# Decode attention beside an MLP: V laid out as K is, P's rows picked by 0/1 products and masked, one sum bank per two batches, wo in two tiles behind V

## The chip, the cores and the metric

The kernel runs on one core of one Trainium2 chip. The metric is the device time of one execution in microseconds (us), the median of the runs shown. Beside it stands one execution that the hardware profiler took; its span is what the profile's pages count from.

## The reference

One decode step (one new token for each of 4 batches, D = 576) through two branches that are added up. Everything is bf16 at the edges.

```python
xn = layernorm(x)                                   # 4 x 576
out = x + A(xn) + B(xn)
# A: attention over the last W = 2048 rows of a cache of 8192
q = (xn @ wq)                                       # 4 x 32 heads x 128
k, v = k_cache[:, :, Sk-W:], v_cache[:, :, Sk-W:]   # 4 x 16 kv heads x 2048 x 128
p = softmax(q . k / sqrt(128))                      # two q heads share a kv head
A = (p . v).reshape(4, 4096) @ wo                   # wo: 4096 x 576
# B: with S = 1 the shifted parts are zero, so w1 and w2 drop out
B = xn + gelu(layernorm(xn) @ w3) @ w4              # w3: 576 x 4608, w4: 4608 x 576
```

K and V of the window are 33.55 MB each, the weights some 20 MB; all of it is read once.

## The kernel before, in words

**Loads.** Nearly every load is issued from SyncE (SP), in one first-in first-out queue. The order: wq; K in eight tiles with w3 and the first 11 of w4's 36 row blocks between the first ones; V; wo; the rest of w4. A pool `big` of four slots of 32 KB per partition holds, one after the other, wq, the K tiles, w3 and its neighbours, V's tiles and w4's end. A load whose slot is still in use waits in SP, and what stands behind it waits too. `k_load` (line 105) brings a K tile as 128 runs of 32 KB: partition 4m + q holds 128 consecutive rows of one of 32 (batch, head) pairs. `v_load` (line 115) brings a pair of heads in two transfers of 128 runs of 16 KB each: partition 32b + p holds 64 consecutive rows of batch b. wo comes in two transfers in runs of 9,216 B (`load_wo`, line 404), the first between V's pairs 1 and 2, the second behind V.

**Scores.** For each K tile VectorE transposes blocks of 32x32 (line 296, four instructions), and TensorE (PE) multiplies (line 303), 32 columns of the array at a time, four such strips side by side. The scores of all 128 rows (32 heads x 4 batches) build up in four PSUM banks S0 to S3, 512 columns each. Beside that stage PE does w3 (line 486) and the first part of w4 (line 394).

**Softmax** (line 308). The maximum of each bank (line 315), their maximum as a bias `nb` (317), exponentials on ScalarE into f32 (320) with row sums, reciprocals (325). P is then scaled by the reciprocals times a 0/1 mask of the batch (lines 339 and 341), transposed on PE (345), and copied into `PZ` (350, 353), where a head's weights lie as 32 columns.

**V.** `v_compute` (line 374) multiplies each head's 64 chunks with PZ: 16 matmuls of 512 columns, in four strips of 32 columns that run side by side, into a bank of its own (383). `head_out` (418) takes the four diagonal blocks out of that bank on VectorE (423, 425); a product with `sel` transposes and sums them (435), and for each four heads products with `pick` (446) and VectorE (454, 455) bring the rows into the order that wo's tile has. wo's products run between the heads (`project`, 459). PE's order in this stage is written out by hand (line 552); the other engines are scheduled by the framework.

**The end.** `merge_sums` (468) folds the partial sums into four accumulators, one for each quarter of the 576 columns; `quads` (413) issues four narrow matmuls for a row block. w4's end arrives last, in ever smaller pieces (570, 502, 577); four copies (594) and two output transfers (596) follow.

Of the kernel before, what the change touches and what calls it, by code (L numbers as in the profile page):

```python
# [20 lines left out]
def kernel(  # L21
# [19 lines left out]
    nc = tc.nc  # L41
# [10 lines left out]
    NCH = W // G  # L52
    NG = P // G
    GK = G // B
    NY = 4
    CP = 16
    NP = NCH // CP
    assert NCH * GK == 512
# [12 lines left out]
    v_win = A_v_cache[:, :, Sk - W:Sk, :]  # L71
# [41 lines left out]
    V_tiles = {}  # L113

    def v_load(pair):
        t = big.tile([P, 2, NCH, Dh], BF16, tag="big", name=f"v{pair}")
        for i in range(2):
            h = 2 * pair + i
            nc.sync.dma_start(out=t[:, i, :, :].rearrange("p c d -> p (c d)"),
                              in_=v_win[:, h].rearrange("b (p c) d -> p b (c d)", p=G))  # L120
            V_tiles[h] = t[:, i, :, :]
# [7 lines left out]
    XR = 8  # L129
    wo_src = A_wo.rearrange("(g p x) n -> p g (x n)", p=P, x=XR)  # L130

# [17 lines left out]
    K_order = [(bp, kq) for bp in range(2) for kq in range(4)]  # L149
    K_tiles = {0: k_load(*K_order[0])}  # L150
# [47 lines left out]
    NH = Hkv * rep  # L198
    qz = pzp.tile([P, 2, NM, NY, G], BF16, tag="pz", name="qz")

    mask = const.tile([P, B], F32)
    nc.vector.tensor_reduce(out=mask[:], in_=ident[:].rearrange("p (h b r) -> p b h r", b=B, r=rep), op=ALU.add, axis=AX.XY)
# [12 lines left out]
    ACCS = [ACC]  # L215
# [66 lines left out]
    S = []  # L282

    def k_scores(n):
# [8 lines left out]
        for i in range(4):  # L293
            e, a = divmod(i, 2)
            c0 = a * C2 // 2
            nc.vector.transpose(out=ap32(kt[e], c0 * 2 * G, [[2 * G, C2 // 2], [1, 2], [2, G]]),  # L296
                                in_=ap32(kn, c0 * 4 * G + e * G, [[4 * G, C2 // 2], [2 * G, 2], [1, G]]))
        for e in range(2):
            for t in range(2):
                y = 2 * e + t  # L300
                for m in range(NM):
                    c = 32 * (m % 4)
                    nc.tensor.matmul(out=S[kq][c:c + 32, :].rearrange("p (c q l) -> p c q l", q=4, l=2),  # L303
                                     lhsT=qz[:, bp, m, y, :], rhs=kt[e][:, :, 4 * m:4 * m + 4, :, t],
                                     start=(bp == 0 and m < 4 and y == 0), stop=(bp == 1 and m >= 4 and y == NY - 1),
                                     skip_group_check=True)

    def softmax():

        E = ktp.tile([P, NCH, NG, GK], F32, tag="kt", name="E")  # L310
        mx = const.tile([P, NG], F32)
        nb = const.tile([P, 1], F32)
        sm = const.tile([P, 2 * NG], F32)
        for g in range(NG):
            nc.vector.reduce_max(out=mx[:, g:g + 1], in_=S[g][:], axis=AX.X)  # L315
        nc.vector.reduce_max(out=nb[:], in_=mx[:], axis=AX.X)
        nc.vector.tensor_scalar_mul(out=nb[:], in0=nb[:], scalar1=-scale)  # L317
        for g in range(NG):
            for x in range(2):
                nc.scalar.activation(out=E[:, :, g, x:GK:2].rearrange("p (c l) q -> p c q l", l=2),  # L320
                                     in_=S[g][:, 256 * x:256 * (x + 1)].rearrange("p (c q l) -> p c q l", q=4, l=2),
                                     func=ACT.Exp, bias=nb[:], scale=scale, accum_out=sm[:, 2 * g + x:2 * g + x + 1])
        rd = const.tile([P, 1], F32)
        nc.vector.tensor_reduce(out=rd[:], in_=sm[:], op=ALU.add, axis=AX.X)
        nc.vector.reciprocal(out=rd[:], in_=rd[:])
        rdm = const.tile([P, B], F32)
        nc.vector.tensor_scalar_mul(out=rdm[:], in0=mask[:], scalar1=rd[:])  # L327

        PZ = pzp.tile([P, Hkv, NCH, B * rep], BF16, tag="pz", name="PZ")
        HC = CP // 2  # L330
        prs = ktp.tile([P, NP, CP, NG, GK, B], BF16, tag="kt", name="prs")
        for piece in range(NP):
            c0 = piece * CP
            pr = prs[:, piece]
            for b in range(B):
                src = E[:, c0:c0 + CP, :, :].rearrange("p c g k -> p (c g k)")
                dst = pr[:, :, :, :, b].rearrange("p c g k -> p (c g k)")
                if b == 3:
                    nc.scalar.mul(out=dst, in_=src, mul=rdm[:, b:b + 1])  # L339
                else:  # L340
                    nc.vector.tensor_scalar_mul(out=dst, in0=src, scalar1=rdm[:, b:b + 1])  # L341
            for half in range(2):
                tp = ps_s.tile([P, HC, P], BF16, tag="S", name=f"pt{piece}{half}")
                for cc in range(HC):
                    nc.tensor.transpose(out=tp[:, cc, :],  # L345
                                        in_=pr[:, half * HC + cc, :, :, :].rearrange("p g k b -> p (g k b)"),
                                        identity=ident[:])
                c1 = c0 + half * HC
                if half:
                    nc.scalar.copy(out=ap_of(PZ, c1 * B * rep, [[NCH * B * rep, Hkv], [B * rep, HC], [1, B * rep]]),  # L350
                                   in_=ap_of(tp, 0, [[B * rep, Hkv], [P, HC], [1, B * rep]]))
                else:
                    nc.vector.tensor_copy(out=ap32(PZ, c1 * B, [[NCH * B, Hkv], [B, HC], [1, B]]),  # L353
                                          in_=ap32(tp, 0, [[B, Hkv], [NH * B // 2, HC], [1, B]]))
        return PZ


    NI = 4
    NB = B * rep
    sel = const.tile([P, NB], F32)  # L360
    nc.vector.tensor_reduce(out=sel[:], in_=ident[:].rearrange("p (q m) -> p m q", m=NB), op=ALU.add, axis=AX.X)
    diag = const.tile([P, NI], F32)
    nc.vector.tensor_reduce(out=diag[:], in_=ident[:].rearrange("p (j i m) -> p i j m", i=NI, m=NB), op=ALU.add,
                            axis=AX.XY)

    pick = const.tile([P, XR, 2, P // XR], BF16)
    for j in range(2):
        nc.vector.tensor_copy(out=pick[:, :, j, :], in_=ident[:].rearrange("p (m x) -> p x m", x=XR))

    half = const.tile([P, 2], F32)  # L370
    nc.vector.tensor_reduce(out=half[:], in_=ident[:].rearrange("p (q j m) -> p j q m", j=2, m=16), op=ALU.add, axis=AX.XY)
    O_tiles = {}

    def v_compute(h):
        bank = ps_o.tile([P, NI * Dh], F32, tag="O", name=f"O{h}")
        vn = V_tiles.pop(h)
        g0, m = divmod(h, NM)
        hp = 4 * (m % 4) + 2 * (m // 4) + g0
        ns = NCH // (NI * NG)
        for s in range(ns):  # L380
            for j in range(NG):
                c0 = (s * NG + j) * NI
                nc.tensor.matmul(out=bank[G * j:G * j + G, :],  # L383
                                 lhsT=PZ[:, hp, c0:c0 + NI, :].rearrange("p c m -> p (c m)"),
                                 rhs=vn[:, c0:c0 + NI, :].rearrange("p c d -> p (c d)"),
                                 start=(s == 0), stop=(s == ns - 1), skip_group_check=True)
        O_tiles[h] = bank

    def acc_matmuls(lhsT, rhs_cols, half):


        for q in range(2):
            o0 = 64 * half + 32 * q
            nc.tensor.matmul(out=ACCS[half][o0:o0 + B, 0:DH], lhsT=lhsT, rhs=rhs_cols(q * DH, (q + 1) * DH),  # L394
                             start=False, stop=False, skip_group_check=True)

    wo_tiles = {}
    groups = {}
    SUMS = []
    NO = 4  # L400

    wo = wop.tile([P, 2, XR, D], BF16)

    def load_wo(g2, n=1):
        s = g2 % 2
        nc.sync.dma_start(out=wo[:, s:s + n].rearrange("p g x n -> p g (x n)"), in_=wo_src[:, g2:g2 + n, :])
        for i in range(n):
            wo_tiles[g2 + i] = wo[:, s + i]

    selects, projects = [], []  # L410
# [7 lines left out]
    def head_out(h):  # L418


        bank = O_tiles.pop(h)
        osum = ktp.tile([P, Dh], F32, tag="kt", name=f"osum{h}")
        nc.vector.tensor_scalar_mul(out=osum[:], in0=bank[:, 0:Dh], scalar1=diag[:, 0:1])  # L423
        for i in range(1, NI):
            nc.vector.scalar_tensor_tensor(out=osum[:], in0=bank[:, i * Dh:(i + 1) * Dh], scalar=diag[:, i:i + 1],  # L425
                                           in1=osum[:], op0=ALU.mult, op1=ALU.add)

        g4, o = divmod(h, NO)

        def transpose_sum():  # L430
            if o == 0:
                OT = ps_tp.tile([P, NO * NB * (1 + XR)], F32, tag="tp", name=f"OT{g4}")
                groups[g4] = OT, small.tile([P, NO, rep, B], BF16, tag="on", name=f"on{g4}")
            OT, on = groups[g4]
# [5 lines left out]
        def select():  # L440
            if o < NO - 1:
                return
# [184 lines left out]
```

## Time and profile before

| what | value |
|---|---|
| median of 3 runs | 212.45 us (212.43 to 212.53) |
| profiled execution, its own time | 212.51 us |
| its span | 210.7 us |
| PE, busy | 99.7 us (47%), 1099 matmuls |
| VectorE (DVE), busy | 128.0 us (61%) |
| ScalarE (ACT), busy | 18.3 us (9%) |
| read from HBM | 87.17 MB, 414 GB/s over the span |

The profile's page divides the span into 40 slices and gives, for each, the busy share of every engine in tenths, the clock that TensorE was granted and the load of the 16 DMA engines. The chain of waits follows the work that ended last back from its end: each piece is what released the next. The timeline lists instructions in order, merged where they repeat, with start, length and count. A window lists for a stretch the busy time and the count of PE, weight loads, DVE, ACT and POOL, then the granted clock (1.00 is full), the DMA engines' busy share and the bytes per time. PE's lengths overlap, since matmuls are pipelined, so a busy PE is not a full one.

### The profile page before, as it was taken

What the parts mean: (1) busy time and instruction counts of PE and PEld (TensorE: products, weight loads), DVE (VectorE), ACT (ScalarE), POOL (GpSimd) and SP (SyncE); (2) the same over time, 40 slices, a digit from 0 to 9 for tenths busy, and PEclk for the clock granted to TensorE, in tenths of its full rate; (3) what the DMA queues carried; (4) which work ended last, traced back from release to release, by engine and by line L of the source; (5) the groups of instructions that cost most, each with busy time, mean ns of one, the idle gap of its engine ahead of it and who ended that gap; (6) DMA issues with size and microseconds to landing.
All of it is one profiled execution on the core that took longest, in us unless ns stands there. A gap on an engine that the chain in (4) does not pass through costs nothing.

```text
span 210.7 us, 2593 instructions
## 1 busy us (share of the span) xinstructions
PE 99.7 (47%) x1099; PEld 50.6 (24%) x1099; DVE 128.0 (61%) x224; ACT 18.3 (9%) x38; POOL 1.8 (1%) x8
## 2 busy tenths in 40 slices
PE   1433159429803333423333330577489455655564
PEld 0110137408301011101111100553234222221352
DVE  7902692096349898979696960996836552522601
ACT  0003200000000000000000008951000000000011
POOL 2100000000000000000000000000000000000000
PEclk9999999999975555555555555589955785555555
DMA  7999999999999999999999999999999999999991
GB/s 299 398 473 423 397 462 395 422 435 470 417 411 473 407 417 467 411 423 460 411 407 426 432 420 414 432 442 423 426 429 426 425 432 417 429 432 411 422 402 60
DMA packets 6002, 87.32 MB, mean 414 GB/s; under 512 B 604, under 2 KB 1128, under 8 KB 1896
## 3 DMA queue, kind: packets, MB, share of 16 engines
q1 hardware_dynamic: 5976, 87.17, 97.3%
q8 instruction: 8, 0.13, 0.2%
q14 instruction: 2, 0.02, 0.0%
q10 hardware_dynamic: 16, 0.01, 0.0%
HBM read 87.17 MB, written 0.00 MB: 414 GB/s over the span
## 4 chain that ended last, share of the span: by engine, by line
DMA 60%; DVE 25%; PE 6%; issue 3%; ACT 3%; SPq 1%; DVEq 0%; ACTq 0%
DMA k<-in_A_k_cache_dram 32%; DVE kt L296 19%; DMA w_end<-in_B_w_dram 16%; DMA v<-in_A_v_cache_dram 12%; PE S L303 4%; DVE prs L341 4%; ACT E L320 2%; PE O L383 1%; DVE PZ L353 1%; PE pt L345 1%; SPq L136 1%; ACT PZ L350 0%; DVE osum L425 0%; SPq L140 0%; PE SUM L415 0%
## 5 line engine op out<-in xcount | busy, mean ns | idle before, releaser
L296 DVE STREAM_TRANSPOSE kt<-k 128x2048 int32<-128x2048 int32 x32 | 71.1, 2281 | 16.2 <-DMA k<-in_A_k_cache_dram 16.1
L303 PE MATMUL S<-kt,qz 128*32 128x512 bf16 x256 | 30.4, 622 | 58.7 <-DVE kt L296 58.7
L383 PE MATMUL O<-v,PZ 128*32 128x512 bf16 x256 | 26.0, 531 | 12.2 <-DMA v<-in_A_v_cache_dram 11.5
L303 PEld LDWEIGHTS <-qz 128*32 128x32 bf16 x256 | 9.4, 126 | 75.6 <-issue 69.2
L423 DVE TENSOR_SCALAR osum<-O,diag 128x128 f32<-128x128 f32 x16 | 5.6, 349 | 23.3 <-PE O L383 23.3
L425 DVE SCALAR_TENSOR_TENSOR osum<-O,diag,osum 128x128 f32<-128x128 f32 x48 | 16.4, 345 | 0.8
L383 PEld LDWEIGHTS <-PZ 128*32 128x32 bf16 x256 | 7.2, 118 | 20.9 <-DMA v<-in_A_v_cache_dram 9.5
L320 ACT ACTIVATE E<-S,nb 128x256 f32<-128x256 f32 x8 | 4.5, 703 | 72.2 <-DVE nb L317 72.2
L345 PE MATMUL pt<-ident,prs 128*128 128x128 bf16 x64 | 6.0, 273 | 9.3 <-DVE prs L341 9.3
L435 PEld LDWEIGHTS OT<-sel,osum 128*128 128x128 f32 x32 | 6.7, 261 | 13.8 <-DVE osum L425 7.9
L435 PE MATMUL OT<-sel,osum 128*128 128x8 f32 x32 | 8.2, 329 | 3.3 <-DVE osum L425 3.3
L345 PEld LDWEIGHTS <-prs 128*128 128x128 bf16 x64 | 5.4, 126 | 10.8 <-ACT prs L339 9.4
L341 DVE TENSOR_SCALAR prs<-E,rdm 128x512 bf16<-128x512 f32 x12 | 7.9, 801 | 0.0
L315 DVE TENSOR_REDUCE mx<-S 128x1 f32<-128x512 f32 x4 | 2.8, 691 | 8.0 <-PE S L303 8.0
L486 PEld LDWEIGHTS <-w3a 128*128 128x128 bf16 x108 | 6.9, 164 | 1.7 <-issue 1.7
L486 PE MATMUL ACC<-ln2T,w3a 128*128 128x4 bf16 x108 | 7.0, 202 | 0.0
L251 DVE CAST q_rows<-qp 128x256 bf16<-128x256 f32 x4 | 1.5, 420 | 8.8 <-PE qp L236 6.7
L394 PE MATMUL ACC<-wo,onx 128*4 128x288 bf16 x48 | 3.4, 434 | 5.6 <-DVE onx L455 5.0
L236 PE MATMUL qp<-wq,xnT 128*8 128x512 bf16 x32 | 3.6, 626 | 3.9 <-DMA wq<-in_A_wq_dram 3.9
L470 ACT COPY sums<-ACC 64x288 f32<-64x288 f32 x1 | 0.4, 392 | 57.0 <-PE ACC L394 57.0
L594 DVE CAST fin<-ACC 4x144 bf16<-4x144 f32 x1 | 0.3, 299 | 7.7 <-PE ACC L415 7.7
L339 ACT ACTIVATE prs<-E,rdm 128x512 bf16<-128x512 f32 x4 | 4.9, 1408 | 0.8 <-DVE rdm L327 0.8
(93 smaller groups left out, 79.0 us busy)
## 6 DMA issues: line engine op xcount, KB each, us to landing
k<-in_A_k_cache_dram SPq DMA_DIRECT2D x8, 4096.0 KB, 29.6
v<-in_A_v_cache_dram SPq DMA_DIRECT2D x16, 2048.0 KB, 25.0
wo<-in_A_wo_dram SPq DMA_DIRECT2D x2, 2304.0 KB, 32.5
wq<-in_A_wq_dram SPq DMA_DIRECT2D x1, 4096.0 KB, 12.7
w3a<-in_B_w_dram SPq DMA_DIRECT2D x1, 2304.0 KB, 26.9
w3b<-in_B_w_dram SPq DMA_DIRECT2D x1, 2304.0 KB
w_end<-in_B_w_dram SPq DMA_DIRECT2D x1, 2016.0 KB, 34.3
w3b<-in_B_w_dram SPq DMA_DIRECT2D x1, 1584.0 KB
```

Source lines behind the costliest of these rows:

```text
L236: nc.tensor.matmul(out=qp[32 * i:32 * i + 2 * B, :], lhsT=x[:, B - B * k:3 * B - B * k], rhs=rhs, start=False, stop=False, skip_group_chec ...
L296: nc.vector.transpose(out=ap32(kt[e], c0 * 2 * G, [[2 * G, C2 // 2], [1, 2], [2, G]]), in_=ap32(kn, c0 * 4 * G + e * G, [[4 * G, C2 // 2], ...
L303: nc.tensor.matmul(out=S[kq][c:c + 32, :].rearrange("p (c q l) -> p c q l", q=4, l=2), lhsT=qz[:, bp, m, y, :], rhs=kt[e][:, :, 4 * m:4 * ...
L320: nc.scalar.activation(out=E[:, :, g, x:GK:2].rearrange("p (c l) q -> p c q l", l=2), in_=S[g][:, 256 * x:256 * (x + 1)].rearrange("p (c q ...
L339: nc.scalar.mul(out=dst, in_=src, mul=rdm[:, b:b + 1])
L341: nc.vector.tensor_scalar_mul(out=dst, in0=src, scalar1=rdm[:, b:b + 1])
L345: nc.tensor.transpose(out=tp[:, cc, :], in_=pr[:, half * HC + cc, :, :, :].rearrange("p g k b -> p (g k b)"), identity=ident[:])
L383: nc.tensor.matmul(out=bank[G * j:G * j + G, :], lhsT=PZ[:, hp, c0:c0 + NI, :].rearrange("p c m -> p (c m)"), rhs=vn[:, c0:c0 + NI, :].rea ...
L423: nc.vector.tensor_scalar_mul(out=osum[:], in0=bank[:, 0:Dh], scalar1=diag[:, 0:1])
L425: nc.vector.scalar_tensor_tensor(out=osum[:], in0=bank[:, i * Dh:(i + 1) * Dh], scalar=diag[:, i:i + 1], in1=osum[:], op0=ALU.mult, op1=AL ...
L435: nc.tensor.matmul(out=OT[:, NB * o:NB * o + NB], lhsT=osum[:], rhs=sel[:], start=True, stop=True, skip_group_check=True)
L486: nc.tensor.matmul(out=gp[:, fc, :], lhsT=lhsT, rhs=rhs, start=False, stop=False, skip_group_check=True)
```

## The change

V is loaded as K is: partition 4m + q holds 128 consecutive rows of a (batch, head) pair, in 32 KB runs, eight tiles of 32 pairs and a quarter of the window each. A chunk c of a V tile thus has 32 pairs on its partitions, and P's weights for it are 64 columns (two heads per pair), zero where row and column belong to different pairs.

- The exponentials go to bf16, unscaled, one instruction per bank (512 columns). 0/1 products with `pick` bring the rows of two batches onto the partitions that V's pairs have (`pick_rows`), ScalarE copies them (`keep_rows`), and VectorE spreads each value over 32 columns and keeps it in its own one by an AND with a mask of all ones or zeros (`spread_rows`). The scaling by batch, the 64 transposes and PZ are gone.
- `v_compute` takes two chunks at a time: 128 weight columns, 256 moving ones, all into one bank per two batches; of the result the two diagonal blocks are used. The last half of the last tile takes single chunks, 64 columns wide, two side by side.
- The scaling by the reciprocals happens once per two batches (`heads_out`), with the reciprocals brought into row order by a product (`reciprocal_rows`); f32 products and a mask bring the rows into wo's order (`heads_rows`, `heads_pick`).
- wo comes in two tiles, in runs of 18,432 B, both behind V and behind the middle of w4. All of wo's products run near the end, with `quads`.
- The bank maxima stand in the source between K's transposes. The hand-written order now covers PE, ScalarE and VectorE.
- The second accumulator of wo and w4 (ACC2) is gone.

The core of the diff:

```diff
-    def v_load(pair):
-        t = big.tile([P, 2, NCH, Dh], BF16, tag="big", name=f"v{pair}")
-        for i in range(2):
-            h = 2 * pair + i
-            nc.sync.dma_start(out=t[:, i, :, :].rearrange("p c d -> p (c d)"),
-                              in_=v_win[:, h].rearrange("b (p c) d -> p b (c d)", p=G))
+    v_rows = A_v_cache.rearrange("b h s d -> (b h) s d")
+    def v_load(n):
+        bp, kq = V_order[n]
+        t = big.tile([P, CK, Dh], BF16, tag="big", name=f"v{n}")
+        lo = Sk - W + kq * 4 * CK
+        src = v_rows[MT * bp:MT * bp + MT, lo:lo + 4 * CK, :].rearrange("m (q c) d -> m q (c d)", q=4)
+        nc.sync.dma_start(out=t[:].rearrange("p c d -> p (c d)"), in_=src)
...
-    XR = 8
-    wo_src = A_wo.rearrange("(g p x) n -> p g (x n)", p=P, x=XR)
+    XR = 16
+    wo_src = A_wo.rearrange("(t p x) n -> p t (x n)", p=P, x=XR)
...
             nc.vector.transpose(out=ap32(kt[e], ...), in_=ap32(kn, ...))
+            if n > 4 and i == 1:
+                bank_max(n - 5)
...
+    def pick_rows(bp, g0, g1):
+        for r in range(rep):
+            ...
+            for q in range(4):
+                nc.tensor.matmul(out=CPS[bp, r][:, g0 * CK:g1 * CK], lhsT=pick[:, bp, r, 3 - q:3 - q + P],
+                                 rhs=EP[:, g0:g1, q, :], start=(q == 0), stop=(q == 3), skip_group_check=True)
+    def keep_rows(bp, g0, g1):
+        for r in range(rep):
+            nc.scalar.copy(out=CB[:, bp, g0:g1, :, r],
+                           in_=CPS[bp, r][:, g0 * CK:g1 * CK].rearrange("p (g c) -> p g c", c=CK))
+    def spread_rows(n):
+        bp, g = V_order[n]
+        X = ktp.tile([P, CK, PB], BF16, tag="kt", name=f"X{n}")
+        src = CB[:, bp, g].rearrange("p c r -> p (c r)").bitcast(I32)
+        for a in range(NX):
+            s32 = src[:, a * CX:(a + 1) * CX]
+            nc.vector.tensor_tensor(out=ap32(X, a * CX * MT, [[MT, CX], [1, MT]]),
+                                    in0=bass.AP(s32.tensor, s32.offset, [list(s32.ap[0]), [1, CX], [0, MT]]),
+                                    in1=ap_of(own, 0, [[0, CX], [1, MT]]), op=ALU.bitwise_and)
+    def v_compute(n, parts=range(NX), narrow=NX):
+        ...
+        for c in range(parts[0] * CX, (parts[-1] + 1) * CX, 2):
+            if c >= narrow * CX:
+                for j in range(2):
+                    nc.tensor.matmul(out=o[PB * j:PB * j + PB, Dh * j:Dh * j + Dh], lhsT=X[:, c + j, :],
+                                     rhs=vn[:, c + j, :], start=False, stop=False, skip_group_check=True)
+            else:
+                nc.tensor.matmul(out=o[:], lhsT=X[:, c:c + 2, :].rearrange("p c n -> p (c n)"),
+                                 rhs=vn[:, c:c + 2, :].rearrange("p c d -> p (c d)"),
+                                 start=(g == 0 and c == 0), stop=False, skip_group_check=True)
...
+        for n in range(1, NV):
+            v_compute(n, narrow=NX // 2 if n == NV - 1 else NX)
+            if n == 1:
+                pick_rows(1, 0, NG)
+                keep_rows(1, 0, NG)
+                reciprocal_rows()
+            if n == 2:
+                merge_sums()
+            if n == 3:
+                heads_out(0)
+            if n + 1 < NV:
+                spread_rows(n + 1)
+            if n == 4:
+                heads_pick(0, heads_rows(0))
+            if n - 1 + NV0 < NV:
+                V_tiles[n - 1 + NV0] = v_load(n - 1 + NV0)
+            if n == NV - NV0 + 1:
+                ...
+                wo.append(load_wo(0, wop, "wo"))
+                wo.append(load_wo(1, big, "big"))
+        heads_out(1)
+        for part in end[:2]:
+            quad_out(*part)
+        heads_pick(1, heads_rows(1))
+        for t in range(NT):
+            for x in range(XR):
+                quads(onx[:, t, x, :], wo[t][:, x, :])
+        for part in end[2:]:
+            quad_out(*part)
```

`heads_rows` is four f32 matmuls of 128 columns, `heads_pick` three VectorE instructions (a product with a 0/1 mask over 512 columns, a reduction, a copy into bf16).

## The prediction

> **What bounds the kernel now.** I read the page's slices first, then the windows by stage, the chain that ended last and the timeline of PE.
>
> ```profile
> span 210.7 us, 2593 instructions
> ...
> PEclk9999999999975555555555555589955785555555
> DMA  7999999999999999999999999999999999999991
> ...
> q1 hardware_dynamic: 5976, 87.17, 97.3%
> ```
>
> The DMA row is full in every slice but the first and the last, and the queue's packets fill 97.3% of the 16 engines' span. So the end is set by 87.17 MB through engines that never rest; a saving on any other engine is worth nothing unless that engine is late at the very end. The chain agrees: its last long pieces are transfers.
>
> ```profile
> 114.67 8.89 DVE kt L296 x4
> ...
> 126.47 0.16 DVE nb L317
> ...
> 126.70 4.56 ACT E L320 x16
> ...
> 148.68 25.04 DMA v<-in_A_v_cache_dram
> 173.72 0.02 issue
> 173.74 33.22 DMA w_end<-in_B_w_dram
> 206.95 0.04 issue
> 207.00 0.28 PE SUM L415
> ```
>
> Columns are start, length, what. The last piece of w4 lands at 206.95, PE ends 1.3 us later, and the span ends 2.5 us after PE, with copies and the output. Two windows compare a stretch of nothing but K with one of nothing but V; two more show what the granted clock does.
>
> ```profile
> 62.00:108.00 46.00, 15.44 (x132) 5.01 (x135) 40.26 (x21) 0.00 (x0) 0.00 (x0) 0.50 1.00 431
> 136.00:192.00 56.00, 36.62 (x372) 17.73 (x369) 32.18 (x109) 4.70 (x5) 0.00 (x0) 0.68 1.01 426
> ...
> 149.10:152.50 3.40, 1.71 (x27) 0.96 (x26) 2.87 (x13) 0.00 (x0) 0.00 (x0) 0.99 1.02 434
> 154.50:161.60 7.10, 7.10 (x62) 2.90 (x58) 3.30 (x11) 0.00 (x0) 0.00 (x0) 0.50 1.02 432
> ```
>
> The last three columns are clock, DMA share and GB/s. With the engines full in both, K (32 KB per partition and transfer) moves at 431 GB/s, V (16 KB) at 426.
>
> **The change, part by part.**
>
> *V's runs.* 16 transfers of 16 KB runs become 8 of 32 KB runs, the shape of K's, in the same slots. 33.55 MB at 426 GB/s are 78.8 us, at 431 GB/s 77.9: **-0.9 us**. The trace's record of single packets says nearly the same: 2048 packets of 16 KB with a median of 613 ns against 1024 of 32 KB with K's 1214 ns, over 16 engines, are 78.5 and 77.7 us (-0.8); by means (617 and 1219 ns) -1.0.
>
> The Trainium skill ("DMA: Bandwidth & Descriptors", Specifications) puts line rate at transfers of 512 B and more; by it both run lengths are at full rate and this part is worth 0. The two windows, 426 and 431 GB/s, disagree with it by 1.2%.
>
> *wo's runs.* 512 packets of 9,216 B (median 352 ns) become 256 of 18,432 B. w3 has packets of that length now: 686 ns. 512 x 352 / 16 = 11.26 us against 10.98: **-0.25 us**, by means -0.2. Both wo tiles move behind V, to where the queue is as full.
>
> *The queue's order.* SP waits for V4's slot (V0 through PE), V5's, and so on. K4 lands at 80.1 by the chain, so K7 lands at 80.1 + 3 x 9.73 (4.19 MB at 431) = 109.3, and V tile n at 119.0 + 9.73 n. wo no longer stands between V1 and V2, so the four tiles that are issued early are used up at 148.2 and V4 must be issued by about 146. V7 lands at 187.1, then w4's middle, wo, w4's end.
>
> *Softmax and P.* Gone: 16 scalings with 0/1 masks, 64 transposes, 8 copies into PZ. The bank maxima stand in the source between K's transposes, but in the built program's order VectorE still has each ahead of the next tile's transposes, as before; so nb is still done at 126.6, and nothing is gained there. New: the first exponential (512 wide; the row for 256 wide is 0.70 us, spaced 0.54; I take 0.8), 4 products of 128 columns per bank, their copies (0.35 each, by 0.375 for 128x256), and the AND, 1024 int32 wide. No row shows an int32 AND. Below, the transposes move 2048 int32 in 2.28 us, 1.1 ns each; above, the product of 144 f32 in 0.31 us is 2.1 ns each with its fixed part. I take 1.2 us, as the fixed part is spread over 1024. A V tile needs four, 4.8 us (at most 8.8), under a landing period of 9.73. The first V matmul then starts at about **130.6**.
>
> *PE in the V stage.* This is where the change adds work: per tile 64 matmuls with 128 weight columns and 256 moving ones, one after the other, where 32 of 512 columns ran four side by side. Rows of PE's timeline:
>
> ```profile
> 134.02 3.61 PE L345 MATMUL pt<-ident,prs 128*128 128x128 bf16 x32 [8.52 <-DVE prs L341]
> ...
> 141.04 1.07 PE L345 MATMUL pt<-ident,prs 128*128 128x128 bf16 x16 [0.31 <-DVE prs L341]
> ...
> 145.72 1.05 PE L383 MATMUL O<-v,PZ 128*32 128x512 bf16 x16
> ```
>
> All three change their weights before each matmul. At full clock 16 of 128 columns take 1.07 us, 67 ns each, or 53 when the latency of one (0.27) is taken off; so 107 to 134 ns for 256 columns. The last row is 4 passes of 512 columns in 1.05: 0.22 each without its latency (0.39), 110 for 256. I take **110 ns**. At half clock (first row) it is 226. Does the clock stay full? Those transposes began at 134.0 and the windows give full clock from 139: 4.8 us at half, and then full while PE was dense.
>
> The sum from 130.6: 480 wide matmuls 52.8; V7's second half as 64 narrow ones, two side by side, 2.6 (40 ns; between the quads' 28 and 57); the picks of P's rows, 8 of 384 and 8 of 512 columns, 3.1; the reciprocals' rows, which PE waits for behind two copies on ScalarE, 1.6 (V2's matmuls are queued behind that wait); the sums' merge 0.5; the f32 products of the first half of the heads 1.5; half of 4.8 us lost to the clock, 2.4. Together 64.5: V7 is done at **195.1**. PE is behind the landings all along, so V4 is asked for at 141 (146 allowed) and no later slot is late.
>
> *The tail.* After V7: 56 quads at 28 ns, 1.6; f32 products 1.5; three steps on VectorE (512 wide, as the 0.69 of L315) 1.75; 128 quads 3.55; 24 quads 0.7. That must end by the landing of w4's last large piece, 206.95 - 1.1 = 205.85; so V7 may be done as late as 205.85 - 9.1 = **196.75**. The slack is 1.65 us, which 508 units of 256 columns use up at 3.3 ns each: the decision point is **113 ns** per matmul, and each ns above it costs 0.5 us. Beyond that the end is as before: the same small w4 pieces, copies and output.
>
> Sum: -0.9 - 0.2 = **-1.1 us**. The profiled execution took 212.51 (span 210.7), 211.4 after; the median shown is 212.45, 0.03% away, so the forecast is 211.4 for both. Cover gone, it is the PE rival's price.
>
> **The rivals.**
>
> *PE sets the end (slower).* The place is V7's end, the price 0.5 us per ns above 113. At the upper end, 134 ns (67 for 128 columns, latency and all), that is +10.5 us, 221.9; I put the likely miss at 120 ns, +3.3: **214.7**. The clock can do it too: every us at half rate loses half a us, so 3.3 us of it use up the slack. For it: the window 149.1 to 152.5 with 1.71 us of work cost the clock, and the next 7 us of gapless work ran at 0.50; if the reciprocals' wait, which leaves some 1.8 us of work in 3.4, did that again for 8 us, PE would lose 4 us, and the end 2.4: 213.8. Against it: the 53 ns that the transposes take without the latency, and 128 full columns in use without a break.
>
> The Trainium skill ("TensorE: Matmul & The Clock Gate", Part 1) has the full clock come back after about 3.4 us of sustained work. By that V0 would lose 1.7 us instead of 2.4; the row of 7.10 us at 0.50 disagrees.
>
> *The rate does not depend on the run's length.* The 5 GB/s would then come from what V's stage does beside the transfers, not from the packets: **212.5**, no change. Against it, the packets' median rates rise with the length across all stages: 9,216 B 26.2 bytes per ns and engine, 16,384 B 26.7, 18,432 B 26.9, 32,768 B 27.0.
>
> *V4 is asked for late.* If the clock stays at half through V0, PE ends it at 130.6 + 64 x 0.226 + 8 x 0.34 = 147.8, 1.8 us after 146: 211.4 + 1.8 = **213.2**, and PE's lateness comes on top.
>
> *The change does not do what it says* in one point, the maxima, counted above. Had they moved, nb would be 4.7 us earlier and PE's slack 6.
>
> **How the numbers follow.** Forecast 0.62 at 211.4 (211.0 to 211.8 by the bounds of the two rates, 210.9 rounded out). PE 0.22, most between 212.5 and 216; no rate gain 0.11; V4 late 0.05. A measurement of this kernel tells some 0.2% (0.4 us) from no change. Faster: 0.62 and 0.02 of slight PE misses. Same, 212.0 to 212.9: 0.11 and 0.02 of PE. Slower: 0.18 and 0.05. The range 210.9 to 214.7 leaves out about 0.1 of PE above and little else.
>
> **What would show it.** Right: V's window at 431 GB/s, w4's last piece landing near 205.9, PE waiting for wo or w4 after V7, V7's matmuls over by 196.8, 7.0 us per tile at a clock near 1. Wrong: a DMA slice under 9 near 150 (V4); wo landed and PE still in its quads (PE), with the pitch or the granted clock telling which; V's window still at 426.

## The result

The changed kernel takes **213.08 us** (median of 9 runs, 212.86 to 213.21) against 212.52 (9 runs, 212.40 to 212.66) for the kernel before: a ratio of 1.0025, interval 1.0015 to 1.0036. It is 0.56 us slower, where 1.1 us faster was forecast. The profiled execution took 213.19 (span 211.4), that of before 212.51 (210.7).

### The profile page after: what moved, and what is told of

Same layout as the page of the kernel before. It is cut to its first block, busy times and chain, and to the rows that moved or that the text cites. A ratio compares the mean times of both kernels' runs of the same rounds, so it can differ in the third digit from the quotient of the medians.

```text
span 211.4 us, 2998 instructions
## 1 busy us (share of the span) xinstructions
PE 121.2 (57%) x1351; PEld 84.1 (40%) x1351; DVE 127.8 (60%) x131; ACT 14.0 (7%) x39; POOL 1.8 (1%) x8
## 3 DMA queue, kind: packets, MB, share of 16 engines
q1 hardware_dynamic: 4568, 87.17, 96.5%
HBM read 87.17 MB, written 0.00 MB: 412 GB/s over the span
## 4 chain that ended last, share of the span: by engine, by line
DMA 44%; PE 28%; DVE 20%; issue 3%; SPq 2%; ACT 1%; DVEq 0%; ACTq 0%
DMA k<-in_A_k_cache_dram 32%; PE O L399 21%; DVE kt L291 19%; DMA w_end<-in_B_w_dram 12%; PE S L300 4%; PE C L363 2%; ACT Z L352 1%; DVE X L381 1%; SPq L131 1%; ACT Z L368 0%; PE OX L429 0%; SPq L135 0%; SPq L492 0%; DVE mx L277 0%; SPq L104 0%
## 5 line engine op out<-in xcount | busy, mean ns | idle before, releaser
L399 PE MATMUL O<-v,X 128*128 128x256 bf16 x480 | 54.9, 277 | 1.7 <-DVE X L381 1.7
L399 PEld LDWEIGHTS <-X 128*128 128x128 bf16 x480 | 47.6, 100 | 8.3 <-DVE X L381 1.9
L381 DVE TENSOR_TENSOR X<-Z,own 128x1024 int32<-128x1024 int32 x32 | 37.0, 1220 | 17.1 <-issue 5.8
L457 PE MATMUL SUM<-wo,onx 128*4 128x144 bf16 x96 | 3.3, 275 | 7.8 <-DMA wo<-in_A_wo_dram 7.8
L352 ACT ACTIVATE Z<-S,nb 128x512 bf16<-128x512 f32 x4 | 2.8, 702 | 72.3 <-DVE nb L540 72.3
L363 PE MATMUL C<-Z,pick 128*128 128x128 bf16 (+2 forms) x24 | 5.3, 374 | 2.1 <-ACT Z L352 2.1
L457 PEld LDWEIGHTS <-onx 128*4 128x4 bf16 x128 | 2.9, 103 | 8.0 <-issue 6.1
L476 PEld LDWEIGHTS <-w3b 128*128 128x128 bf16 x72 | 4.5, 163 | 0.8 <-issue 0.8
L476 PE MATMUL ACC<-ln2T,w3b 128*128 128x4 bf16 x72 | 4.6, 202 | 0.0
L368 ACT CAST Z<-C 128x128 bf16<-128x128 f32 (+2 forms) x6 | 3.2, 542 | 17.6 <-PE C L363 17.3
```

Of the source, the lines that this page charges most:

```text
L352: nc.scalar.activation(out=EP[:, g].rearrange("p q (c l) -> p c q l", l=2), in_=S[g][:].rearrange("p (c q l) -> p c q l", q=4, l=2), func= ...
L363: nc.tensor.matmul(out=CPS[bp, r][:, g0 * CK:g1 * CK], lhsT=pick[:, bp, r, 3 - q:3 - q + P], rhs=EP[:, g0:g1, q, :], start=(q == 0), stop= ...
L368: nc.scalar.copy(out=CB[:, bp, g0:g1, :, r], in_=CPS[bp, r][:, g0 * CK:g1 * CK].rearrange("p (g c) -> p g c", c=CK))
L381: nc.vector.tensor_tensor(out=ap32(X, a * CX * MT, [[MT, CX], [1, MT]]), in0=bass.AP(s32.tensor, s32.offset, [list(s32.ap[0]), [1, CX], [0 ...
L399: nc.tensor.matmul(out=o[:], lhsT=X[:, c:c + 2, :].rearrange("p c n -> p (c n)"), rhs=vn[:, c:c + 2, :].rearrange("p c d -> p (c d)"), sta ...
L457: nc.tensor.matmul(out=SUMS[q][32 * q:32 * q + B, 0:DQ], lhsT=lhsT, rhs=rows[:, q * DQ:(q + 1) * DQ], start=False, stop=False, skip_group_ ...
```

## The profile after

The same lines of the page as for before, and one more, the queue of instruction fetches (packets, MB, share of 16 engines):

```profile
span 211.4 us, 2998 instructions
...
PEclk9999999999975555555555555699999999999958
DMA  7999999999999999999999999999999999999980
...
q1 hardware_dynamic: 4568, 87.17, 96.5%
q8 instruction: 10, 0.16, 0.3%
```

That last line in the page of before:

```profile
q8 instruction: 8, 0.13, 0.2%
```

The DMA row is still at 9 from the second slice up to the last two, where `91` has become `80` (these slices begin 0.6 to 0.7 us later than before, so the windows below are the fairer comparison). The transfers' share fell from 97.3 to 96.5%, although no slice before the end is less full. And where 8 packets brought instructions, there are now 10.

The chain that ended last (start, length, what):

```profile
130.70 3.59 PE O L399 x16
...
136.31 12.23 PE O L399 x112
...
174.29 7.00 PE O L399 x64
...
183.10 25.52 DMA w_end<-in_B_w_dram
...
208.67 0.33 PE SUM L457 x4
```

PE now carries the middle of the chain, as forecast (7.00 us per V tile), but the end still belongs to a transfer, w4's last and smallest piece, in place at 208.62. Five windows of the changed kernel, with the columns that the prediction's windows have:

```profile
62.00:108.00 46.00, 15.23 (x132) 4.92 (x135) 40.26 (x21) 0.00 (x0) 0.00 (x0) 0.50 1.00 432
130.70:137.70 7.00, 7.00 (x39) 4.83 (x40) 4.08 (x4) 1.67 (x4) 0.00 (x0) 0.65 1.00 431
136.00:192.00 56.00, 54.92 (x506) 47.78 (x506) 34.03 (x33) 4.17 (x10) 0.00 (x0) 1.00 1.00 428
188.00:193.00 5.00, 5.00 (x83) 4.44 (x82) 0.00 (x0) 0.00 (x0) 0.00 (x0) 1.00 1.05 442
200.00:205.00 5.00, 0.63 (x36) 0.47 (x28) 0.00 (x0) 0.00 (x0) 0.00 (x0) 0.55 0.93 370
```

The clock was half for the first 4.9 us of V's matmuls and full after that (0.65 over 7 us), V's stage moved 428 GB/s, and V7's matmuls ran without a pause at full clock. The last window is the odd one. In the kernel before it reads:

```profile
200.00:205.00 5.00, 2.86 (x88) 2.42 (x88) 0.30 (x2) 0.79 (x2) 0.00 (x0) 0.50 1.01 413
```

There the engines were full until 205; now 7% of their time is empty, while w4's last pieces are still under way. PE did not cause that. It waited for wo (total, times, longest):

```profile
PE SUM L457 <- DMA wo<-in_A_wo_dram: 7.8, 2, 4.4
```

**Where the time went.** The trace has every packet's start and length, though not its engine. Of packets above 600 B in the last stage (instruction fetches among them), so many are in flight at each moment, that is, so many of the 16 engines are still at work:

| us | 203.6 | 204.1 | 204.6 | 205.1 | 205.6 | 206.1 | 206.6 | 207.1 |
|---|---|---|---|---|---|---|---|---|
| before | 16 | 16 | 10 | 9 | 9 | 4 | 0 | 0 |
| after | 16 | 10 | 9 | 8 | 3 | 2 | 2 | 2 |

After the change nearly every engine finishes earlier, and two finish later than any did before. A transfer is 128 packets. The steps of this table fit eight for each engine; then a transfer is complete when its slowest engine is. The mean end of the 16 (200 us plus the number in flight, summed over time, divided by 16; what overlaps at a hand-over is not counted twice) went from 205.46 to 205.00, and the end of the last large packet of w4 from 206.46 to 207.33. The engines' mean gained 0.46 us; the latest one's lag behind that mean grew from 1.00 to 2.33, and 1.33 - 0.46 = 0.87 us is what the end lost. The execution lost 0.68 of it.

## Theory and rivals

**Theory: instruction fetches.** Each fetch in these two traces is a packet of 16 KB that lasts 0.94 to 1.11 us, and between two of them PE does 127 matmuls on average before the change and 122 after it (with their weight loads, about 250 instructions of PE), in single intervals 64 to 181. In the kernel before they start at 33.7, 50.0, 69.2, 111.5, 145.0, 158.0, 182.3 and 204.6; in the changed one at 33.8, 50.3, 69.5, 113.1, 142.4, 158.1, 172.8, 185.7, 196.4 and 203.3. Right behind seven of the ten (three of the eight before, where most fall beside shorter packets) a 32 KB data packet takes about 1.7 us in place of 1.22; with the fetch itself, an engine loses some 1.6 us. As no engine is ever idle, it cannot catch up. Eight fetches put about half of the engines 1.6 us behind (the table's step from 16 to 9); two more, for the 252 added matmuls, fall on engines that already have one, and put those 1.6 us behind again.

The trace shows the times and lengths; that the ninth falls on an engine that already has one is inferred from when the engines end. With a large packet behind which no other starts taken as an engine's end, the 16 ends of the changed kernel lie in three groups: eight up to 204.80, six from 205.38 to 205.73, two at 207.26 and 207.33. Ten fetches that go round eight engines leave just that: eight engines without one, six with one, two with two. In the kernel before there are two groups, seven up to 204.90 and nine from 205.91; eight fetches account for eight of the nine. The trace of that kernel also has an 8 KB packet of another instruction queue at 168.0, which the changed one lacks; whether it made the ninth engine late was not tried.

**Rival 1:** the work or the order behind V sets the end. **Rival 2:** 32 KB packets are coarser, so the engines end more raggedly.

## The experiments

In the table, "fetches" counts those that started before w4's last large packet ended. All kernels read the same 87.17 MB.

| kernel | matmuls | fetches | mean end | latest end | lag | median us |
|---|---|---|---|---|---|---|
| before | 1099 | 8 | 205.46 | 206.46 | 1.00 | 212.52 |
| before + 96 tiny | 1195 | 8 | 205.60 | 206.41 | 0.81 | 212.51 |
| before + 176 tiny | 1275 | 9 | 205.78 | 207.78 | 2.00 | 213.81 |
| before + 256 tiny | 1355 | 10 | 205.70 | 207.60 | 1.90 | 213.90 |
| after | 1351 | 10 | 205.00 | 207.33 | 2.33 | 213.08 |
| after, again | 1351 | 10 | 204.98 | 207.17 | 2.19 | 213.16 |
| after, less of V | 1127 | 8 | 204.85 | 205.82 | 0.97 | 212.22 |
| the same + 224 tiny | 1351 | 10 | 204.93 | 207.18 | 2.25 | 213.14 |
| after, V in 16 KB runs | 1351 | 10 | 205.53 | 207.81 | 2.28 | 213.66 |
| after, fewer instructions | 1163 | 9 | 205.27 | 206.94 | 1.67 | 212.94 |
| the same, early pick | 1171 | 9 | 204.76 | 207.15 | 2.39 | 214.58 |

### The kernel before with 256 tiny matmuls

Products of zeros, 8 columns wide, added to a sum in K's stage, where PE waits anyway: instructions without work. 64 behind each of K's tiles 2 to 5.

```diff
         k_scores(n)
+        for i in range(64 if 2 <= n < 6 else 0):
+            nc.tensor.matmul(out=ACC[0:B, 0:8], lhsT=zeros[:, 0:B], rhs=zeros[:, 0:8], start=False, stop=False,
+                             skip_group_check=True)
```

> The kernel before with 256 matmuls of 4x8 zeros added into ACC in K's stage (64 after each of K tiles 2 to 5, where PE idles): 512 more instructions on PE and nothing else. Theory (program fetches): the instruction queue has 10 packets of 16 KB instead of 8, two of the 16 DMA engines carry two of them, and w4's last pieces wait for these: +1.5 to +1.8 us, 214.0 to 214.3. Rival (wo behind V and the tail's order cost the time in the changed kernel): no change, 212.5. Rival (fetches only take bandwidth from all engines alike): 2 x 1.6 / 16 = +0.2 us, 212.7.

Measured: 213.90, a ratio of 1.0065 (1.0053 to 1.0077), with 10 fetches. Neither V's layout nor any work behind V was touched, and the kernel lost 1.4 us. Rival 1 cannot say why.

### The same with 96, and with 176

The edit is the one above, with 48 behind tiles 2 and 3, then with 44 behind tiles 2 to 5.

> The same with 96 tiny matmuls (48 after each of K tiles 2 and 3), 192 more instructions: 9 packets of 16 KB. Theory (program fetches that go round eight engines, so that the ninth falls on an engine that has one): +1.5 to +1.8 us, as with ten, 214.0 to 214.3. Rival (each fetch past the eighth adds its own part): half of what ten add, 213.3. Rival (bandwidth): 212.6.

> The kernel before with 176 tiny matmuls (44 after each of K tiles 2 to 5), 352 more instructions: 9 packets of 16 KB, the ninth at about 195 to 203 us, while transfers still run (with 96 it came at 207.2, after the last of them, and cost nothing). Theory, fetches go round eight engines: the ninth falls on an engine that has one, +1.3 to +1.5 us, 213.8 to 214.0, as with ten. Rival, any of the 16 engines can get it: a fresh one, 212.5. Rival, each costs its own part: 213.2.

96: 212.51 (one of the 12 executions took 214.19, which no trace explains), ratio 1.0007 (0.9994 to 1.0019), where 1.5 us more was expected. 176: 213.81, 1.0048 (1.0036 to 1.0060). The pages' DMA row and fetch queue, for 96 and for 176:

```profile
DMA  7999999999999999999999999999999999999992
...
q8 instruction: 9, 0.15, 0.3%
```

```profile
DMA  7999999999999999999999999999999999999990
...
q8 instruction: 10, 0.16, 0.3%
```

With 96, a ninth fetch did come, at 207.2, when the last large packet (206.41) was through; no engine had anything left to delay. It costs nothing there, and neither did the 96 instructions themselves. With 176 the ninth came at 200.6 and the tenth at 208.6. So one fetch more, in time to meet data, costs the whole 1.2 us, and one engine is left working alone: it ends at 207.78, the other 15 by 206.52. (The rows' last digits, `92` and `90`, do not show this by themselves, since the last slice begins at 205.4 in the one and at 206.8 in the other.) The expectation for 96 counted fetches and forgot to ask when they start.

### The changed kernel with less of V

It leaves out every second pair of chunks in V tiles 1 to 6 and does the last tile wide: 224 matmuls fewer, all transfers kept. The second kernel puts 224 tiny matmuls into K's stage (56 behind tiles 2 to 5).

```diff
-        for c in range(parts[0] * CX, (parts[-1] + 1) * CX, 2):
+        for c in range(parts[0] * CX, (parts[-1] + 1) * CX, 4 if 0 < n < 7 else 2):
...
-            v_compute(n, narrow=NX // 2 if n == NV - 1 else NX)
+            v_compute(n)
```

> The changed kernel with every second pair of chunks of V tiles 1 to 6 left out of the products, and the last tile in wide matmuls alone: 224 matmuls (448 instructions) fewer on PE, all transfers as they were. Theory (program fetches): 8 packets of 16 KB, no DMA engine carries two, w4's last pieces land some 1.7 us earlier: 211.2 to 211.6. Rival (tail's order): 213.1, since no transfer and no wait at the end changes. Rival (bandwidth): 212.9.

> The run before this one with 224 tiny matmuls put back in K's stage (56 after each of K tiles 2 to 5): V's products still left out in part, but as many instructions on PE as in the changed kernel. Theory (program fetches): 10 packets again, 212.9 to 213.3. Rival (the lighter V stage is what helped in the run before): as fast as that run, 211.4.

Less of V: 212.22, ratio 0.9981 (0.9973 to 0.9990). With the tiny ones: 213.14, 1.0029 (1.0018 to 1.0041). Their pages, in that order:

```profile
DMA  7999999999999999999999999999999999999991
...
q8 instruction: 8, 0.13, 0.3%
```

```profile
DMA  7999999999999999999999999999999999999980
...
q8 instruction: 10, 0.16, 0.3%
```

This is the pair that decides. With PE's work of V cut by more than a third, the time with ten fetches (213.14) is that of the full changed kernel (213.08, 213.16): what PE computes in V's stage does not set the end. With eight fetches it is 0.92 us less, the lag is that of the kernel before, 0.97 against 1.00, and the engines end in two groups of eight (up to 204.88 and up to 205.82). But the gain over before is 0.3 us, not the 0.9 to 1.3 expected. Part of the difference lies outside the profiled span: the device time exceeds the span by 1.8 to 2.7 us in this kernel, by 1.7 to 1.9 in the other kernels of the table. By the medians of the spans it is 210.1 with eight fetches and 211.35 with ten, against 210.7 before, a gain of 0.6 us. What the added time outside the span is, no run shows.

### The changed kernel with V in 16 KB runs

```diff
-        nc.sync.dma_start(out=t[:].rearrange("p c d -> p (c d)"), in_=src)
+        H = CK * Dh // 2
+        for i in range(2):
+            nc.sync.dma_start(out=t[:].rearrange("p c d -> p (c d)")[:, i * H:(i + 1) * H],
+                              in_=src[:, :, i * H:(i + 1) * H])
```

> The changed kernel with each V tile in two transfers of 16 KB runs instead of one of 32 KB, PE untouched. Theory (the run's length sets the rate): +0.8 to +1.0 us on the changed kernel, 213.9 to 214.1. Rival (the length is worth nothing): 213.1.

Measured: 213.66, ratio to before 1.0045 (1.0032 to 1.0058). The mean end moved by 0.53 us (205.00 to 205.53); the time moved by 0.5 to 0.6, or by 0.3 to 0.5 when each kernel is set against the kernel before in its own series, with intervals that overlap. The lag stayed (2.28). So the run length is worth about 0.5 us of V, not 0.9, and shorter packets do not bring the engines closer: rival 2 falls. The edit doubles the number of transfers too, and the two were not tried apart.

### The kernel before with 896 tiny matmuls

128 behind each of K's tiles 1 to 7, to see whether the loss stops once every engine has a fetch.

> The kernel before with 896 tiny matmuls (128 after each of K tiles 1 to 7), 1792 more instructions: 15 packets of 16 KB. Theory, round eight engines, none with more than two: as with ten, 213.8 to 214.1. Rival, every packet past the eighth on the same one or two engines: three or more on one, 215.4 to 217. Rival, bandwidth of all alike: +7 x 1.6 / 16 = 213.2.

Measured: 228.32, ratio 1.0725. Inconclusive: so many matmuls held up K's stage, and the queue ran dry twice, as the page's row of GB/s in 40 slices shows:

```profile
GB/s 281 466 391 449 417 455 396 422 463 414 423 446 411 440 429 414 452 160 373 394 408 423 429 416 438 434 426 402 15 227 411 429 420 424 429 426 419 426 406 56
```

After such a gap the engines can start level again, so the lag at the end is not that of 15 fetches.

### The changed kernel with fewer PE instructions, twice

All work is kept, in 376 and 360 fewer instructions: the last V tile wide, w3's tail for both halves in one product, the heads' products in bf16, and wo and w4's end in two products of 288 columns instead of four of 144, without the merge of the sums and with one copy at the end instead of four. The first kernel also picks P's rows of the first two batches in one go; the second keeps the early pick of the changed kernel. The core:

```diff
-            v_compute(n, narrow=NX // 2 if n == NV - 1 else NX)
+            v_compute(n)
...
-                quads(onx[:, t, x, :], wo[t][:, x, :])
+                acc_matmuls(onx[:, t, x, :], lambda a, z, t=t, x=x: wo[t][:, x, a:z])
```

> The changed kernel with all its work but some 350 instructions fewer on PE: the last V tile in wide matmuls, the picks of the first two batches in one go, w3's tail for both halves at once, the heads' products in bf16, and wo and the rest of w4 in two matmuls a row block instead of four, without the merge of sums. Theory (program fetches): the ninth packet comes after the last transfer or not at all, 211.6 to 212.2, faster than both kernels. Rival (tail's order): 213.1 or later, since wo and w4 come in the same order.

> The seventh kernel with the early pick of the first 256 rows of P restored as in the changed kernel (16 more PE instructions, about 2337 in all). Fetch theory: 9 fetches, the ninth at 205 to 207 and so nearly free, V0's matmuls from about 130.7 again, no gap of the DMA queue near 146; w4's last large piece near 205.9 on its latest engine, and a time of 211.6 to 212.2, under both the kernel before (212.5) and the changed one (213.1). Rival, that PE's new work or the order behind V sets the end and not the fetches: 212.9 to 213.2, as the changed kernel.

> The changed kernel itself on the same chip, so that the kernel above is compared with it as directly as with the kernel before. All theories: 212.9 to 213.3, ten fetches.

The first: 212.94 (12 runs, 212.34 to 214.37), ratio 1.0021 (1.0003 to 1.0038). The second: 214.58, 1.0097 (1.0084 to 1.0111). The changed kernel on the same chip as the second: 213.16, 1.0031. Both are misses, each for a reason of its own. In the first, the pick in one go holds V0 back; its windows 128 to 136 and 144 to 148, and below them the same two of the changed kernel:

```profile
128.00:136.00 8.00, 4.26 (x12) 1.50 (x12) 1.98 (x2) 3.54 (x9) 0.00 (x0) 0.50 0.95 410
144.00:148.00 4.00, 4.00 (x39) 3.59 (x37) 4.00 (x4) 0.00 (x0) 0.00 (x0) 1.00 0.99 381
```

```profile
128.00:136.00 8.00, 6.26 (x32) 3.90 (x30) 4.63 (x4) 2.74 (x9) 0.00 (x0) 0.52 0.98 422
144.00:148.00 4.00, 4.00 (x39) 3.59 (x37) 2.39 (x3) 0.00 (x0) 0.00 (x0) 1.00 0.95 410
```

PE did 12 matmuls in the first window instead of 32, and V4 was asked for at 143.9 instead of 141.6. Around 146 there is then a small gap: for 1.5 us only 13 to 15 packets are in flight, where the changed kernel has 16, and eleven packets that start between 145.8 and 147.5 take 1.4 to 2.9 us instead of 1.22; the window shows 381 GB/s against 410. The kernel's times are spread over 2 us, which no run explains. In the second kernel it is the tail. The chain, and one window:

```profile
179.18 25.40 DMA wo<-in_A_wo_dram
...
204.62 4.90 PE ACC L443 x50
209.52 0.27 PE ACC L602 x4
```

```profile
204.60:209.60 5.00, 4.98 (x54) 2.99 (x53) 0.00 (x0) 0.00 (x0) 0.00 (x0) 0.66 0.21 72
```

PE starts on wo's second tile at 204.62 (204.67 in the changed kernel), but the products, in two strips instead of four and at a mean clock of 0.66 after PE's wait of 4.4 us, take longer: 3.27 us for that tile, where the changed kernel's quads take 2.1 at a clock that is little higher (0.73), and 1.85 for w4's pieces behind it. PE ended the kernel, and the fetches were not tested by it: its last large packet ended at 207.15, with the ninth fetch at 202.4, not at 205 to 207. No full version here beats the kernel before. What the less-of-V kernel reached (212.22, or 0.6 us by its span) shows how little there was to win.

## Why the prediction was wrong

**The step that failed** is in the tail: "Beyond that the end is as before: the same small w4 pieces, copies and output", with w4's last large piece landing 1.1 us earlier, at 205.85. That piece's last packet was to move from 206.46 to about 205.4, and came at 207.33. The part that counted the cost of the change in PE time (480 wide matmuls, 64 narrow ones, 64.5 us) was close, 63.0 us from V's first matmul to its last, and it was taken as the whole cost of PE's work. But 252 more matmuls are also 504 more instructions, these are two more packets of 16 KB through the same full engines, and both land, by the groups above, on engines that are among the late ones already: +1.33 us on the lag, which is not in the sum at all. The eight fetches stood in the page of before, as `q8 instruction: 8`.

**The rate term was too large.** -0.9 for V and -0.25 for wo: the packets' own times did shrink as read (V 1218.6 ns per 32 KB against 2 x 615.7; wo 691 against 2 x 351.4; over 16 engines -0.8 and -0.2). But V by itself is worth 0.5 at the end (V in 16 KB runs), and with equal fetches the mean end gained 0.61 (less of V). V's window shows 428 GB/s, not the 431 that I took from K's. The two windows were not alike: K's holds one fetch in 46 us, V's three in 56, and at some 1.6 us of one engine each that is, by estimate, 1.4 of the 5 GB/s between them. The packets' lengths promise too much as well: in the record a packet begins 3 to 4 ns before the one that it follows ends. Up to 200 us these overlaps add up to 0.89 us per engine before and 0.66 after, since the longer runs have fewer hand-overs, so 0.23 of the 1.0 us were counted that could not be gained. (The time with fewer than 16 packets in flight did not grow; it is 0.07 us per engine in both.) Why the rest, about 0.2, did not arrive is open.

**What held.** V's first matmul: forecast 130.6, came at 130.70. The AND: 1.2 us, measured 1.22. The pitch of V's matmuls: 110 ns, measured 109.2; a tile 7.0 us, measured 7.00. The clock: half for 4.8 us, measured 4.9. V7 done: 195.1, measured 193.7, since the narrow matmuls took 28 ns, not 40, and the waits were shorter. V4 was not late: it was asked for at 141.6 (forecast 141), and no slice is under 9 before the end. That the measured 213.1 lies beside the price of that rival, 213.2, is chance. PE then waited for wo, as "What would show it" asked. So the rival that I gave most chance, PE, did not happen, and that of no rate gain only by half. The sign came from a mechanism that was in none of the rivals; the forecast's "a saving on any other engine is worth nothing" was read as if a cost there were worth nothing too.

**By how much the sum now closes.** Rate -0.46 on the mean (two more fetches in it), lag +1.33: +0.87 at the last large packet; 0.68 measured between the profiled executions, 0.56 between the medians. The 0.2 to 0.3 between are in the small pieces and products behind it, and are not taken apart.

## What to carry to other kernels

In a kernel whose DMA engines never rest, count instructions as well as their time: each 16 KB of program is a packet on one of those engines, and the kernel ends with the engine that is furthest behind, not with the mean. Look at the instruction queue in the profile's list of queues, and at whether the last transfers end together; if some engines end early, bytes are no longer what bounds the end. A count of fetches is not enough: one that starts after the last large packet is free.

## What the runs showed of the hardware

- **Program fetches happen during the run.** One packet of 16,384 B per about 250 instructions of PE, 0.88 to 1.22 us long in all the traces, and a delay of some 1.6 us for one engine. The Trainium skill ("Trainium Architecture — The Big Picture", The software stack) gives instructions 64 bytes, with which 16,384 B are 256 of them; the traces agree. The same section of the Trainium skill has the streams moved into the engines when the program is loaded; in these runs 8 to 15 packets of instructions came between 33 us and the end.
- **The ninth is the dear one.** From 8 to 9 fetches the lag went from 0.8 to 1.0 us to 2.0, and the tenth added nothing (1.9). Nine fetches that meet data leave one engine ending alone (207.78 behind 206.52 with 176 tiny matmuls, 207.15 behind 205.40 with the early pick); ten leave two, in each of the five traces that have ten in time. That fits a rotation over eight engines; the trace does not name engines, so it is inferred.
- **Run length counts beyond 16 KB.** Halving V's runs from 32 to 16 KB (with twice the transfers) moved the mean end by 0.53 us of V's 78. By the Trainium skill's line rate from 512 B ("DMA: Bandwidth & Descriptors", Specifications) it would cost nothing. Measured, it costs 0.7%, and the measurement stands.
